# Gated linear attention and a mixture of experts: the first unit in parts, gate steps without a buffer, a carry by a product, constant products at the start, and a table of due times

## The chip, the cores and the metric

The kernel runs on one core of a Trainium2 chip. The core has five engines with a queue each: PE (TensorE: matrix products and transpositions, with weight loads shown as an engine of their own, PEld), DVE (VectorE), ACT (ScalarE, with tables of functions that have to be loaded), POOL (GpSimd) and SP (SyncE, which here only issues transfers). An engine takes its instructions strictly in the order of its queue and waits on semaphores. The metric is the device time of one execution in microseconds (us), the median of several runs.

## The reference

Attention first: for each of 4 batches and 8 heads a complex decay multiplies a 48 x 48 state at each of 768 steps, and k v^T is added to its real part.

```python
mag = np.sqrt(a_re * a_re + a_im * a_im)
scale = np.minimum(mag, 0.999) / (mag + 1e-06)
a_re_n, a_im_n = (a_re * scale, a_im * scale)
for t in range(S):
    new_re = ar * S_re - ai * S_im
    new_im = ar * S_im + ai * S_re
    S_re, S_im = (new_re + kv, new_im)
    y[:, :, t] = np.einsum('bhd,bhde->bhe', q[:, :, t], S_re)
```

The result, as 3072 rows of 384, goes through a layer of 8 experts (384 to 1024 to 384), of which each row uses the one with the largest logit:

```python
logits = x @ w_gate
expert_idx = np.argmax(logits, axis=1)
h = np.maximum(x_sorted[lo:hi] @ w1[e], 0.0)
y_sorted[lo:hi] = h @ w2[e]
return (gate_w[:, None] * y).astype(np.float32)
```

`gate_w` is the softmax probability of the chosen expert. All is float32.

## The kernel before

**Attention.** The 768 steps are cut into 6 units `u` of 128 (NU), which lie on the partitions. A unit has 4 batches (B), so there are 24 pairs g = 4 u + b; a half is two batches (HB). 384 = 8 heads x 48 is one batch's row, 768 a half's, 1536 a unit's. The decay is kept as logarithm and angle. For each unit:

- `load_gates` brings a_re and a_im (`ar`, `ai`), `load_qkv` a half of q, k and v, all from SP.
- `gate_steps` turns them into the clipped logarithm (`ar`) and the ratio (`ai`) in four steps s0 to s3: six passes on ACT (Relu, Ln, Exp, Square, Ln, Exp, all but Relu and Square bound to one ACT table) and four on DVE. Buffers `A` and `R` are single.
- `decay` sums the logarithm over the unit's steps by a product with the triangular matrix `tri` (tile `csl`) and takes its exponential both ways (`E`, `Ei`).
- `angle` takes the arctangent, under the other ACT table. For u > 0 an accumulating transfer from POOL adds the angle at the end of the unit before (`cd`, in DRAM) to row 0. `turns` sums the angles by a product with `tri_turn` (tile `cst`), keeps the fraction of a turn (`fg`), and sends its last row through DRAM, a scaling on DVE and DRAM again to `cd` for the next unit. `rotation` takes sines (`CS`).
- `products` multiplies q and E to `Qe`, k and Ei to `Ke` (a half at a time), and those by CS to `Q` and `K` (a batch at a time).
- `scores(u, b, hg)`, for four heads: transposes K and Q (`tp`), copies them on ACT (`kt`, `qt`), multiplies them (`at`) and masks on DVE (`am`). `outer` forms k v^T (`dk`), `state` carries the state `G` on, `results` forms the output (`yt`) from `am` with v and `qt` with G, `evict` copies it (`ys`), `finish` turns it back (`xb`, with the logits), and stores it to `xd`.

**What sets the order.** Each instruction gets a priority when it is written, `cur_priority`, and a scheduler builds one fixed order for every engine from priorities and dependencies. `put(t, f)` writes f at the due time t, in pairs: `tc.cur_priority = 2000 + int(t * 200)`. Before the change unit 0's gate steps are due from -8, by halves; the decay of unit 0 and all four steps of unit 1 come next, then the table of the angles, then unit 0's turns and sines. In the loop over g, `ahead(g)` places the preparation of unit u + 1 and the first steps of unit u + 2 beside the attention of unit u, with one set of due times for all units; attention's own are products -1.2, scores 0 and 0.3, outer 0.5, results 0.7 and 0.9, evict 1.1, finish 1.3, state 1.5.

**Experts.** `route`, `places` and what follows sort the rows by expert. For each expert `gather` fetches its rows (`xg`, indirect transfers on POOL), `turn` transposes them (`tp`, copied to `xt`), `expert` multiplies with w1 (`hps`, then `ht`) and w2 (`yps`), scales (`y`) and scatters to the output. Weights are loaded two experts ahead by `load_w`. The sizes are the constants CAPS. `in_range` checks that the gates lie where the fast path holds: it loads a_re and a_im once more (`rc`) and compares on DVE (`junk`). `early` runs part of expert 0 under the last unit.

Of the kernel before, what the change touches and what calls it, by code (L numbers as in the profile page):

```python
# [20 lines left out]
P = 128  # L21
# [15 lines left out]
def kernel(  # L37
# [57 lines left out]
    nc.vector.memset(ones, 1.0)  # L95
    mhalfpi = const([P, 1], "mhalfpi")
# [55 lines left out]

    T["ops"] = []

    def act(**kw):

        ins = nc.scalar.activation(**kw)  # L157
        behind(ins, [T["table"]])
        T["ops"].append(ins)

# [7 lines left out]
    def load_gates(u, half):  # L168
        for nm, src in (("ar", a_re), ("ai", a_im)):
            if half == 0:  # L170
                T[nm, u] = ga.tile([P, B, H, D], FP, tag=nm, name=nm)
            sl = slice(half * HB, (half + 1) * HB)
            nc.sync.dma_start(  # L173
                out=T[nm, u][:, sl], in_=src[sl, :, u * P : (u + 1) * P, :].rearrange("b h t d -> t b h d")
            )
# [12 lines left out]
    def gate_steps(u, b0, b1):  # L188

        if b0 == 0:  # L190
            T["A", u] = ga.tile([P, B, H, D], FP, tag="A", name="A", bufs=1)
            T["R", u] = ga.tile([P, B, H, D], FP, tag="R", name="R", bufs=1)
        ar, ai, A, R = (flat(T[nm, u][:, b0:b1]) for nm in ("ar", "ai", "A", "R"))

        def s0():
            act(out=A, in_=ar, func=AF.Relu, bias=a_low)
            act(out=A, in_=A, func=AF.Ln, bias=a_min)

        def s1():
            act(out=R, in_=A, func=AF.Exp, scale=-1.0)  # L200
            tt(out=ai, in0=ai, in1=R, op=OP.mult)
            ts(out=ai, in0=ai, scalar1=-T_MAX, scalar2=T_MAX, op0=OP.max, op1=OP.min)

        def s2():
            act(out=R, in_=ai, func=AF.Square)
            act(out=R, in_=R, func=AF.Ln, bias=1.0)
            stt(out=A, in0=R, scalar=0.5, in1=A, op0=OP.mult, op1=OP.add)

        def s3():
            act(out=R, in_=A, func=AF.Exp, scale=-1.0, bias=ln_eps)  # L210
            stt(out=ar, in0=A, scalar=LN_CAP, in1=R, op0=OP.min, op1=OP.subtract)  # L211
# [3 lines left out]
    def decay(u, half):  # L215

        cs = psC.tile([P, HB, DM], FP, tag="cs", padded_shape=[P, HB, 512], name="csl")
        for c in range(HB):
            mm(cs[:, c], tri, T["ar", u][:, half * HB + c].rearrange("p h d -> p (h d)"))
        for nm, sc in (("E", 1.0), ("Ei", -1.0)):  # L220
            t = ch.tile([P, HB, DM], FP, tag=nm, name=nm, bufs=3)
            act(out=t, in_=cs, func=AF.Exp, scale=sc)
            T[nm, u, half] = t
# [18 lines left out]
    def turns(u, half):  # L242

        fg = un.tile([P, HB, H, 2, D], FP, tag="fg", name="fg")
        T["fg", u, half] = fg
        cs = psC.tile([P, HB, H, D], FP, tag="cs", padded_shape=[P, HB, 8, 64], name="cst")
        prev = T["mm"]
        for c in range(HB):
# [3 lines left out]
        r, f = fg[:, :, :, 0, :], fg[:, :, :, 1, :]  # L252
        ts(out=r, in0=cs, scalar1=MAGIC, scalar2=MAGIC, op0=OP.add, op1=OP.subtract)
        tt(out=f, in0=cs, in1=r, op=OP.subtract)
        fi = fg.bitcast(I32).rearrange("p b h a d -> p (b h) a d")
        ts(out=fi[:, :, 0, :], in0=fi[:, :, 1, :], scalar1=0x7FFFFFFF, scalar2=None, op0=OP.bitwise_and)
        if u + 1 < NU:
# [11 lines left out]
    def rotation(u, half):  # L269

        fg = T["fg", u, half].rearrange("p b h a d -> p (b h) a d")
        CS = un.tile([P, HB * H, 2, D], FP, tag="CS", name="CS", bufs=3)
        act(out=CS[:, :, 0], in_=fg[:, :, 0], func=AF.Sin, scale=2.0 * math.pi, bias=mhalfpi)
        act(out=CS[:, :, 1], in_=fg[:, :, 1], func=AF.Sin, scale=2.0 * math.pi)
        T["CS", u, half] = CS

    def products(u, b):
        half, c = divmod(b, HB)
        for nm, src, dec in (("Q", "q", "E"), ("K", "k", "Ei")):
            if c == 0:  # L280
                e = ch.tile([P, HB * H, D], FP, tag=nm + "e", name=nm + "e", bufs=1)
                tt(
                    out=e.rearrange("p h d -> p (h d)"),
                    in0=flat(T[src, u, half]),
                    in1=T[dec, u, half].rearrange("p b x -> p (b x)"),
                    op=OP.mult,
                )
                T[nm + "e"] = e
# [305 lines left out]
    def expert(i, t0, t1, psH, psO, yp):  # L594
# [14 lines left out]
        for t in range(t0, t1):  # L609
            n = min(P, CAPS[i] - t * P)  # L610
# [30 lines left out]
    def put(t, f, *a):  # L641
        tc.cur_priority = 2000 + int(t * 200)
# [12 lines left out]
    load_qkv(0, 1, "v")  # L655
# [5 lines left out]
    for half in range(2):  # L661
        load_gates(2, half)
    table("natural_log_exp_and_others")
    for i, fs in enumerate(zip(gate_steps(0, 0, HB), gate_steps(0, HB, B))):
        for f in fs:
            put(-8 + i, f)
    for half in range(2):
        put(-4, decay, 0, half)
    for i, fs in enumerate(zip(gate_steps(1, 0, HB), gate_steps(1, HB, B))):
        for f in fs:  # L670
            put(-3, f)
    put(-3, table, "trig_and_small")
    for half in range(2):
        put(-3, angle, 0, half * HB, (half + 1) * HB)
        put(-2.5 + half, turns, 0, half)
    for half in range(2):
        put(-2 + half, rotation, 0, half)
    put(-1, angle, 1, 0, B)

    def ahead(g):  # L680

        u, b = divmod(g, B)
        n, m = u + 1, u + 2
        X = n * B
        if n >= NU:
# [399 lines left out]
```

## Time and profile before

| | us |
|---|---|
| median of 3 runs (588.27, 580.65, 583.8) | 583.8 |
| the profiled execution | 584.5 |
| its span on the core | 582.7 |
| first transposition of K starts | 51.40 |
| first product of expert 0 with all its rows starts | 317.08 |

The span runs from the first instruction to the last and is what the profile divides. One more view is of use, the busy tenths of 40 equal slices of the span (14.6 us each; 9 is 90% or more; PEclk is the clock that TensorE was granted):

```profile
PE   0327999999899999999997999999999999999993
PEld 0114888887788798888775655555555555565651
DVE  3356977868887777776367345302203131110210
ACT  6766978788477665533310110111101011000000
POOL 2000000000000000001044031402213021101001
PEclk9999999999999999999998999999999999999997
```

The first three to four slices are preparation, slices 4 to 19 attention, and from slice 21 on the experts run, with DVE and ACT nearly idle. A busy PE is not PE at its peak: in attention the weight loads (PEld) are busy for 70 to 90% of a slice, in the experts for about half.

### The profile page before, as it was taken

Reading aid. Unit: us, or ns where it says so; the run is one execution under the profiler, and the core shown is the slowest. Engines: PE = TensorE matmul, PEld = TensorE weight load, DVE = VectorE, ACT = ScalarE, POOL = GpSimd, SP = SyncE. Lnnn points to the kernel's source line nnn. Section 1 sums busy time; section 2 is a strip of 40 time slices with the busy share of each in tenths; the row PEclk is TensorE's granted clock in tenths of the full one; section 3 lists DMA queues with packets and bytes.
Section 4 is the critical chain, followed back from the end, with each engine's and each line's share of the span. In section 5 each row is a group of like instructions: output and inputs, shape, how many; then the busy total and the mean of one; then the engine's idle time right before and its main releaser. Section 6 shows DMA issues by size and latency. Waiting matters only on the chain.

```text
span 582.7 us, 8024 instructions
## 1 busy us (share of the span) xinstructions
PE 521.9 (90%) x3133; PEld 365.2 (63%) x3133; DVE 283.6 (49%) x574; ACT 217.8 (37%) x322; POOL 67.3 (12%) x94
## 2 busy tenths in 40 slices
PE   0327999999899999999997999999999999999993
PEld 0114888887788798888775655555555555565651
DVE  3356977868887777776367345302203131110210
ACT  6766978788477665533310110111101011000000
POOL 2000000000000000001044031402213021101001
PEclk9999999999999999999998999999999999999997
DMA  9934574765574737203539985522335232330000
GB/s 167 208 58 56 106 133 89 154 110 110 111 119 76 145 76 139 42 28 105 196 124 355 372 318 229 181 85 69 147 133 164 109 103 92 131 118 28 10 14 28
DMA packets 166727, 73.41 MB, mean 126 GB/s; under 512 B 148398, under 2 KB 159704, under 8 KB 166681
## 3 DMA queue, kind: packets, MB, share of 16 engines
q1 hardware_dynamic: 163096, 63.14, 44.3%
q0 software_dynamic: 3584, 9.68, 4.7%
q8 instruction: 26, 0.43, 0.3%
q14 instruction: 21, 0.16, 0.1%
HBM read 63.27 MB, written 9.74 MB: 125 GB/s over the span
## 4 chain that ended last, share of the span: by engine, by line
PE 81%; SPq 5%; ACT 4%; DVE 4%; DMA 2%; issue 1%; POOL 0%; DVEq 0%; ACTq 0%
PE hps L67 22%; PE yps L67 21%; PE at L67 8%; PE yt L67 7%; PE tp L300 7%; PE dk L67 4%; PE xb L67 4%; PE cst L67 3%; SPq L173 2%; DMA rc<-in_a_im_dram 2%; PE csl L67 2%; SPq L182 2%; PE tp L573 2%; ACT R L157 1%; PE sp L67 1%
## 5 line engine op out<-in xcount | busy, mean ns | idle before, releaser
L67 PE MATMUL hps<-xt,wa 128*128 128x416 f32 (+7 forms) x432 | 134.2, 470 | 2.8 <-DVE xt L580 2.8
L67 PE MATMUL yps<-wb,ht 128*128 128x384 f32 (+6 forms) x464 | 133.9, 487 | 0.0
L67 PEld LDWEIGHTS hps<-xt,wa 128*128 128x128 f32 x432 | 81.2, 194 | 49.8 <-issue 21.3
L67 PEld LDWEIGHTS yps<-wb,ht 128*128 128x128 f32 (+6 forms) x464 | 75.1, 175 | 56.0 <-issue 8.6
L618 DVE TENSOR_SCALAR y<-yps,gate 128x384 f32<-128x384 f32 (+2 forms) x24 | 14.8, 617 | 111.8 <-PE yps L67 111.8
L606 ACT ACTIVATE ht<-hps 128x416 f32<-128x416 f32 (+7 forms) x36 | 16.8, 467 | 131.1 <-PE hps L67 114.3
L67 PE MATMUL at<-qt,kt 96*128 96x128 f32 x384 | 55.0, 283 | 0.7 <-ACT qt L302 0.7
L608 DVE TENSOR_SCALAR ht<-hps 128x416 f32<-128x416 f32 (+7 forms) x36 | 18.9, 525 | 69.8 <-PE hps L67 69.4
L585 POOL DMA_INDIRECT out_dram<-y,row x29 | 29.1, 1005 | 198.5 <-DVE y L618 173.6
L67 PEld LDWEIGHTS at<-qt,kt 96*128 96x128 f32 x384 | 47.8, 191 | 6.6 <-ACT qt L302 2.7
L308 DVE TENSOR_TENSOR am<-at,tri 128x512 f32<-128x512 f32 x48 | 33.0, 687 | 22.8 <-PE at L67 22.7
L67 PE MATMUL yt<-am,v 128*48 128x128 f32 x384 | 40.5, 282 | 3.2 <-DVE am L308 3.0
L67 PE MATMUL csl<-ar,tri 128*128 128x384 f32 x48 | 23.2, 590 | 21.1 <-DVE ar L211 15.6
L554 POOL DMA_INDIRECT xg<-xd,tok x29 | 30.4, 1050 | 94.4 <-PE tp L300 50.1
L302 ACT COPY kt<-tp 96x512 f32<-96x512 f32 x48 | 27.9, 581 | 33.9 <-PE tp L300 33.8
L300 PE MATMUL tp<-ident,K 128*96 128x128 f32 x192 | 35.8, 284 | 2.6 <-ACT kt L302 2.0
L67 PE MATMUL cst<-ai,tri_turn 128*128 128x384 f32 x48 | 21.1, 561 | 15.9 <-ACT ai L157 13.7
L67 PE MATMUL yt<-qt,G 96*48 96x128 f32 x320 | 35.1, 274 | 0.0
L628 ACT COPY z<-yps 32x384 f32<-32x384 f32 (+3 forms) x13 | 6.1, 470 | 73.3 <-PE yps L67 73.3
L67 PE MATMUL dk<-v,K 128*96 128x48 f32 x320 | 31.2, 248 | 0.6 <-DVE G L339 0.6
L67 PEld LDWEIGHTS dk<-v,K 128*96 128x96 f32 x320 | 30.4, 167 | 2.1 <-issue 0.9
L300 PE MATMUL tp<-ident,Q 128*96 128x128 f32 x192 | 31.0, 277 | 0.0
(148 smaller groups left out, 634.2 us busy)
## 6 DMA issues: line engine op xcount, KB each, us to landing
wa<-in_moe_w_dram SPq DMA_DIRECT2D x8, 1536.0 KB, 6.4
wb<-in_moe_w_dram SPq DMA_DIRECT2D x8, 1536.0 KB, 11.5
ar<-in_a_re_dram SPq DMA_DIRECT2D x12, 384.0 KB, 4.6
ai<-in_a_im_dram SPq DMA_DIRECT2D x12, 384.0 KB
q<-in_q_dram SPq DMA_DIRECT2D x12, 384.0 KB, 4.7
k<-in_k_dram SPq DMA_DIRECT2D x12, 384.0 KB, 4.4
v<-in_v_dram SPq DMA_DIRECT2D x12, 384.0 KB, 4.8
xd<-x SPq DMA_DIRECT2D x24, 192.0 KB, 3.8
```

The lines of the kernel that those rows point to most:

```text
L67: T["mm"] = nc.tensor.matmul(o, lhsT=lhsT, rhs=rhs, start=start, stop=stop, skip_group_check=True)
L173: nc.sync.dma_start(out=T[nm, u][:, sl], in_=src[sl, :, u * P : (u + 1) * P, :].rearrange("b h t d -> t b h d"))
L182: nc.sync.dma_start(out=t, in_=src[sl, :, u * P : (u + 1) * P, :].rearrange("b h t d -> t b h d"))
L300: nc.tensor.transpose(out=tp[0:DD, j], in_=X[:, hg * 4 + j], identity=ident)
L302: nc.scalar.copy(out=t[0:DD], in_=tp[0:DD])
L308: tt(out=am, in0=at, in1=bc(tri, 1, 4), op=OP.mult)
L554: nc.gpsimd.indirect_dma_start(out=T["xg", i][0:n, t], out_offset=None, in_=xd[0:rows, :], in_offset=bass.IndirectOffsetOnAxis(ap=tok[0:n, ...
L573: ins = nc.tensor.transpose(out=tp[:, (t - t0) * P : (t - t0) * P + n], in_=xg[0:n, t, d * P : (d + 1) * P], identity=ident[0:n, 0:n],)
L585: nc.gpsimd.indirect_dma_start(out=out, out_offset=bass.IndirectOffsetOnAxis(ap=row[0:n, i, t : t + 1], axis=0), in_=y[0:n], in_offset=Non ...
L606: nc.scalar.activation(out=ht[:, f, c0:c1], in_=ps, func=AF.Relu)
L608: ts(out=ht[:, f, c0:c1], in0=ps, scalar1=0.0, scalar2=None, op0=OP.max)
L618: ts(out=y[0:n], in0=ps[0:n], scalar1=g, scalar2=None, op0=OP.mult)
```

## The change

1. Unit 0 is loaded and prepared in three parts: batch 0, batch 1, half 1. `decay`, `turns`, `rotation` and `products` take a range of batches. In unit 0 a maximum on DVE replaces the Relu on ACT (`c0`); later units keep the Relu.
2. `gate_steps` works in `ar` and `R` (two buffers); `A` is gone, `Square` stands in s1 and is not bound to a table. `E` and `Ei` have four buffers instead of three.
3. Unit 1's carry is a product of `last` (ones in its last row) with unit 0's `fg`, accumulated into `cst`. Units 2 to 5 keep the way through DRAM.
4. `warm` writes 40 products of `tri` with itself ahead of unit 0's turns, in ten groups that each wait for an ACT pass.
5. The table `WHEN` gives each piece a due time for each unit, relative to the unit's first pair, and `put` starts at 4000.
6. In the experts, `turn(i + 1)` is written within `expert(i)`, ahead of its last two tiles of `yps`, and the second expert's weights are loaded ahead of its gather.

```diff
+    last = const([P, P], "last")
+    nc.gpsimd.affine_select(
+        out=last, in_=ones, pattern=[[0, P]], base=-(P - 1), channel_multiplier=1, compare_op=OP.is_ge, fill=0.0
+    )
...
+    def warm(n):
+
+        w = psX.tile([P, P], FP, tag="xb", padded_shape=[P, 512], name="warm")
+        for i in range(n):
+            ins = mm(w, tri, tri)
+            if i == 0:
+                tc.add_manual_dep(ins.ins, T["act"].ins.name, SYNC, reason="pace")
...
-            T["A", u] = ga.tile([P, B, H, D], FP, tag="A", name="A", bufs=1)
-            T["R", u] = ga.tile([P, B, H, D], FP, tag="R", name="R", bufs=1)
-        ar, ai, A, R = (flat(T[nm, u][:, b0:b1]) for nm in ("ar", "ai", "A", "R"))
+            T["R", u] = ga.tile([P, B, H, D], FP, tag="R", name="R", bufs=2)
+        ar, ai, R = (flat(T[nm, u][:, b0:b1]) for nm in ("ar", "ai", "R"))
 
         def s0():
-            act(out=A, in_=ar, func=AF.Relu, bias=a_low)
-            act(out=A, in_=A, func=AF.Ln, bias=a_min)
+            if T["when"](f"c{u}"):
+                ts(out=R, in0=ar, scalar1=A_MIN, scalar2=None, op0=OP.max)
+                act(out=ar, in_=R, func=AF.Ln)
+            else:
+                nc.scalar.activation(out=R, in_=ar, func=AF.Relu, bias=a_low)
+                act(out=ar, in_=R, func=AF.Ln, bias=a_min)
 
         def s1():
-            act(out=R, in_=A, func=AF.Exp, scale=-1.0)
+            act(out=R, in_=ar, func=AF.Exp, scale=-1.0)
             tt(out=ai, in0=ai, in1=R, op=OP.mult)
             ts(out=ai, in0=ai, scalar1=-T_MAX, scalar2=T_MAX, op0=OP.max, op1=OP.min)
+            T["act"] = nc.scalar.activation(out=R, in_=ai, func=AF.Square)
...
-        if u > 0:
+        if u > 1:
             nc.gpsimd.dma_start(
...
-        for c in range(HB):
-            mm(cs[:, c], tri_turn, T["ai", u][:, half * HB + c].rearrange("p h d -> p (h d)"))
+        for c in range(c0, c1):
+            mm(cs[:, c], tri_turn, T["ai", u][:, half * HB + c].rearrange("p h d -> p (h d)"), True, u != 1)
             if u > 0:
                 behind(T["mm"], [prev])
+            if u == 1:
+                mm(cs[:, c], last, T["fg", 0, half][:, c, :, 1], False, True)
...
-        if u + 1 < NU:
+        if 0 < u < NU - 1:
...
+            if t == t1 - 2 and between is not None:
+                between()
...
+    WHEN = {
+        "l1": 0, "l2": 1, "p0": 2, "p1": 4, "p2": 4, "p3": 2, "p4": 4, "p5": 3, "s0.0.0": -8.68, "c0": True,
...
+        "results0": 1.02, "results1": 1.04, "state": 1.61, "evict": 1.11, "scores0": -0.86, "scores1": 0.42,
+        "outer": 0.43, "finish": 1.53, "products": -1.42, "LE2": -6.28, "d2.0": -3, "d2.1": 0.0, "h3": False,
...
-    load_gates(0, 0)
-    load_gates(0, 1)
-    load_gates(1, 0)
-    load_gates(1, 1)
-    load_qkv(0, 0, "qk")
-    load_qkv(0, 1, "qk")
-    load_qkv(0, 0, "v")
-    load_qkv(0, 1, "v")
+    HS = [(0, HB), (HB, B)]
+    for b0, b1 in ((0, 1), (1, HB), (HB, B)):
+        load_gates(0, b0, b1)
+    order = [(load_qkv, 0, 0, "qk"), (load_qkv, 0, 0, "v"), (load_qkv, 0, 1, "qk"), (load_qkv, 0, 1, "v")]
+    order.insert(when("l1"), (load_gates, 1, 0, HB))
+    order.insert(when("l2"), (load_gates, 1, HB, B))
...
+    turn(0, EARLY, tiles(0), psG)
+    load_w(1, T["turned"])
     for i in range(E):
         t0 = EARLY if i == 0 else 0
-        turn(i, t0, tiles(i), psG)
         if i + 1 < E:
             gather(i + 1, 0, tiles(i + 1))
-        if i == 0:
-            load_w(1, T["turned"])
-        expert(i, t0, tiles(i), psH, psO, yp)
+        expert(i, t0, tiles(i), psH, psO, yp, (lambda: turn(i + 1, 0, tiles(i + 1), psG)) if i + 1 < E else None)
```

**Where instructions stand now.** PE from the start of the program, before (the first row is the branch that starts the queue; `x4` is four in a row):

```order
L1080 UNCONDITIONAL_BRANCH
L67 MATMUL csl<-ar,tri 128x384 x4
L67 MATMUL cst<-ai,tri_turn 128x8x48 x4
L67 MATMUL csl<-ar,tri 128x384 x2
L300 MATMUL tp<-ident,K 96x128 x4
L300 MATMUL tp<-ident,Q 96x128 x4
L67 MATMUL dk<-v,K 96x48 x8
```

The same place after:

```order
L67 MATMUL warm<-tri 128x128 x3
L67 MATMUL csl<-ar,tri 128x384
L67 MATMUL warm<-tri 128x128 x5
L67 MATMUL csl<-ar,tri 128x384
L67 MATMUL warm<-tri 128x128 x32
L67 MATMUL cst<-ai,tri_turn 128x8x48 x4
L326 MATMUL tp<-ident,K 96x128 x4
L326 MATMUL tp<-ident,Q 96x128 x4
```

Of the six `csl` products ahead of the first transposition two are left, for unit 0's first half; the other four stand behind it, and the constant products are new. On ACT, around the first table of sines, before (`ai<-ai` is the arctangent, `CS<-fg` a sine; `A<-A,a_min` to `R<-A,ln_eps` are unit 1's gate steps):

```order
L157 ACTIVATE A<-A,a_min 128x768 x2
L157 ACTIVATE R<-A 128x768 x2
L157 ACTIVATE R<-ai 128x768 x2
L157 ACTIVATE R<-R 128x768 x2
L157 ACTIVATE R<-A,ln_eps 128x768 x2
L162 ACT_TABLE_LOAD
L157 ACTIVATE ai<-ai 128x768 x2
L157 ACTIVATE ai<-ai 128x1536
L157 ACTIVATE CS<-fg 128x16x48
```

And after, where copies for attention stand between the sines:

```order
L175 ACT_TABLE_LOAD
L169 ACTIVATE ai<-ai 128x384
L218 ACTIVATE R<-ai 128x768
L169 ACTIVATE ai<-ai 128x384
L169 ACTIVATE ai<-ai 128x768
L169 ACTIVATE ai<-ai 128x1536
L169 ACTIVATE CS<-fg,mhalfpi 128x8x48
L169 ACTIVATE CS<-fg 128x8x48 x2
L328 COPY kt<-tp 96x512
L328 COPY qt<-tp 96x512
L169 ACTIVATE CS<-fg,mhalfpi 128x8x48
L328 COPY kt<-tp 96x512
```

The last two steps (s2, s3) of unit 0's second half and of unit 1, with their `csl` products and exponentials, moved from ahead of the first transposition to behind it. PE within unit 2, before (numbers tell tiles apart; `at_1343` is masked to `am_1348`):

```order
L300 MATMUL tp_1439<-ident_65,K_1416 96x128 x4
L67 MATMUL at_1343<-qt_1341,kt_1334 128x128 x4
L300 MATMUL tp_1446<-ident_65,Q_1412 96x128 x4
L67 MATMUL yt_148<-am_1348,v_763 48x128 x2
L67 MATMUL yt_148<-qt_1341,G1_944 48x128 x2
```

After, a place of the same kind (`at_1206` is masked to `am_1211`):

```order
L326 MATMUL tp_1213<-ident_65,K_1169 96x128 x4
L67 MATMUL at_1206<-qt_1204,kt_1197 128x128 x4
L326 MATMUL tp_1220<-ident_65,Q_1165 96x128 x4
L67 MATMUL yt_150<-am_1211,v_825 48x128
L326 MATMUL tp_1353<-ident_65,K_1330 96x128 x4
L326 MATMUL tp_1360<-ident_65,Q_1328 96x128 x4
L67 MATMUL at_1227<-qt_1225,kt_1218 128x128 x4
L67 MATMUL yt_150<-am_1211,v_825 48x128
```

The pair's transpositions now run further ahead of the results, so that other products stand between `at` and the `yt` that need its mask. DVE where the early part of expert 0 ends (`junk` is the range check, two passes to a check), before:

```order
L618 TENSOR_SCALAR y_3081<-yps_3080,gate_154 128x384
L580 COPY xt_3026<-tp_3136 128x192
L777 SCALAR_TENSOR_TENSOR junk_3411,inr_3135<-rc1_3408,rc0_3407 128x1536 x2
L777 SCALAR_TENSOR_TENSOR junk_3567,inr_3135<-rc1_3564,rc0_3563 128x1536
L618 TENSOR_SCALAR y_3095<-yps_3094,gate_154 128x384
L580 COPY xt_3026<-tp_3144 128x192
```

After:

```order
L647 TENSOR_SCALAR y_3140<-yps_3139,gate_156 128x384
L606 COPY xt_3085<-tp_3195 128x192
L860 SCALAR_TENSOR_TENSOR junk_3489,inr_3194<-rc1_3486,rc0_3485 128x1536 x2
L647 TENSOR_SCALAR y_3154<-yps_3153,gate_156 128x384
L606 COPY xt_3085<-tp_3203 128x192
```

The first pass of the second check moved from ahead of the copy to `xt` to behind it. PE at the boundary of experts 4 and 5, before:

```order
L67 MATMUL yps_3824<-wb_3561,ht_3755 128x384 x8
L67 MATMUL yps_3838<-wb_3561,ht_3755 16x384 x8
L573 MATMUL tp_3880<-ident_65,xg_3745 128x128 x3
L573 MATMUL tp_3885<-ident_65,xg_3745 128x128 x3
L573 MATMUL tp_3890<-ident_65,xg_3745 128x128 x3
L67 MATMUL hps_3906<-xt_3879,wa_3715 128x384 x3
```

After:

```order
L599 MATMUL tp_3884<-ident_65,xg_3804 128x128 x3
L599 MATMUL tp_3889<-ident_65,xg_3804 128x128 x3
L67 MATMUL yps_3899<-wb_3639,ht_3814 128x384
L599 MATMUL tp_3894<-ident_65,xg_3804 128x128 x3
L67 MATMUL yps_3899<-wb_3639,ht_3814 128x384 x7
L67 MATMUL yps_3913<-wb_3639,ht_3814 16x384 x8
L67 MATMUL hps_3965<-xt_3883,wa_3793 128x384 x3
```

The transpositions of the next expert's rows stand ahead of the last two tiles of `yps`.

More of the change, by code (lines that the diff above doesn't have):

```diff
@@ L660 @@
             )
[L661 to L675, printed above, removed]
@@ L680, in ahead, with sine @@
+    def sine(n):
+        X = n * B
+        put(X + when(f"TR{n}"), table, TR)
+        if not ANG.get(n):
+            put(when(f"a{n}") + X, angle, n, 0, B)
+        for half in range(2):
+            put(X + when(f"t{n}.{half}"), turns, n, half)
+            put(X + when(f"r{n}.{half}"), rotation, n, half)
+        if n + 1 < NU and STEPS[n] > 1:
+            ANG[n + 1] = True
+            put(X + 4 + when(f"a{n + 1}"), angle, n + 1, 0, B)
     def ahead(g):
         u, b = divmod(g, B)
-        n, m = u + 1, u + 2
@@ L684, in ahead @@
[L684 to L708 removed]
+        n = u + 1
@@ L710, in at @@
+        if n < NU and b == 0:
+            log_exp(n)
+        if n < NU and b == (0 if n == 1 else 1):
+            if u in GROUPS:
+                put(n * B + when(f"g{u}"), T["second"])
+            sine(n)
     def at(t, f, g, *a):
@@ L712, in at @@
             put(g + t, f, *divmod(g, B), *a)
-    at(-1.2, products, 0)
     at(0, scores, 0, 0)
```

180 lines of the change are left out of this document (108 added, 72 removed), and 16 rows, old and new, of the table WHEN.

## The prediction

> **What bounds the kernel now.** I read the page's first part, then busy time by stretch (columns: stretch and length; busy us and count of PE, weight loads PEld, DVE, ACT, POOL; granted clock; DMA share; GB/s). The cuts are the first transposition, the second unit's first K product and the end of attention; the last row is one dense slice.
>
> ```profile
> span 582.7 us, 8024 instructions
> PE 521.9 (90%) x3133; PEld 365.2 (63%) x3133; DVE 283.6 (49%) x574; ACT 217.8 (37%) x322; POOL 67.3 (12%) x94
> ```
>
> ```profile
> 0.00:51.40 51.40, 14.34 (x20) 6.07 (x21) 24.42 (x40) 32.16 (x38) 3.52 (x31) 1.00 0.94 138
> 51.40:84.00 32.60, 31.02 (x265) 26.46 (x263) 24.88 (x34) 27.72 (x38) 1.09 (x1) 1.00 0.56 93
> 84.00:287.10 203.10, 195.81 (x1852) 165.11 (x1852) 152.00 (x306) 130.26 (x188) 5.24 (x6) 1.00 0.52 109
> 204.00:224.00 20.00, 20.00 (x216) 18.35 (x214) 15.56 (x38) 11.25 (x19) 0.76 (x1) 1.00 0.39 75
> ```
>
> For 51.4 us PE has almost nothing; ACT, the busiest, prepares two units of gates. From 51.4 to 84 ACT is busy 85% and DVE 76%: they feed the first unit. After that PE is first in line. Next the timeline at the start (start, duration, engine, line, operation, idle time before).
>
> ```profile
> 4.92 0.93 ACT L157 ACTIVATE A<-ar,a_low 128x768 f32<-128x768 f32 x1 [2.91 <-DMA ar<-in_a_re_dram]
> 7.72 0.96 DVE L201 TENSOR_TENSOR ai<-ai,R 128x768 f32<-128x768 f32 x1 [5.47 <-ACT R L157]
> 8.94 0.55 DVE L202 TENSOR_SCALAR ai<-ai 128x768 f32<-128x768 f32 x1
> 19.67 0.79 ACT L157 ACTIVATE E<-csl 128x768 f32<-128x768 f32 x1
> 20.36 0.80 ACT L157 ACTIVATE Ei<-csl 128x768 f32<-128x768 f32 x1
> 35.63 1.28 ACT L162 ACT_TABLE_LOAD   x1
> 42.98 2.90 PE L67 MATMUL cst<-ai,tri_turn 128*128 128x384 f32 x4 [2.24 <-DVE fg L254]
> 51.40 1.06 PE L300 MATMUL tp<-ident,K 128*96 128x128 f32 x4
> 83.12 0.94 DVE L291 TENSOR_TENSOR K<-CS,Ke 128x768 f32<-128x768 f32 x1
> ```
>
> The last row is the K product of pair 4 (second unit, first batch). It is the yardstick: in both orders the same preparation lies behind it (gates of unit 2 done, those of unit 3 not begun).
>
> **Term 1, the first unit in parts.** Prices, by form:
>
> ```profile
> L157 ACT ACTIVATE R<-A 128x1536 f32<-128x1536 f32 x4 | 6.0, 1491 | 0.0
> L157 ACT ACTIVATE R<-A 128x768 f32<-128x768 f32 x4 | 3.3, 840 | 0.1
> L302 ACT COPY kt<-tp 96x512 f32<-96x512 f32 x48 | 27.9, 581 | 33.9 <-PE tp L300 33.8
> L157 ACT ACTIVATE E<-csl 128x768 f32<-128x768 f32 x12 | 9.7, 812 | 4.5 <-PE csl L67 4.4
> ```
>
> 768 more elements cost ACT 0.65 us, so a pass over 384 is about 0.52 us (estimate). Ahead of the first batch's sines ACT now has 18 passes of 384, 12 of 768, one of 1536 and one table load: 18 x 0.5 + 12 x 0.85 + 1.5 + 1.3 = 22.0. A load of half the size should land about 1 us sooner than at 4.9, and the maximum that replaces the Relu is on DVE: start 4.3. Three waits for a pair of DVE passes (as 7.72 and 8.94 show them, about half as long) add 2.5: sines done at about 29. DVE, with two Ke parts and the second batch's turns ahead, then makes Q and K at 0.94 each: first transposition at 32, 19 us earlier. The load order, the added mask on POOL and the loads of unit 2 behind the second half's turns on SP are covered by that wait: no one needs them before 40.
>
> But work stays behind it. From 29.4 to the sines of pair 4 ACT's order holds 20 copies (0.58 less the 0.1 by which neighbours overlap: the E pass at 19.67 takes 0.79, and the next starts 0.69 later), 3 copies of 384 elements (0.37 by the slope above), six E and Ei at 0.71, sines 4.0 (two of 384, four of 768), six passes of 768 at 0.8, six of 1536 at 1.43, two table loads 2.6: 9.6 + 1.1 + 4.3 + 4.0 + 4.8 + 8.6 + 2.6 = 35.0 us. At the 80% to which ACT and DVE fill the stretch they bound (85 and 76 above) this takes 43.7: sines at 73.1, then two DVE products and a queue of about 1: K of pair 4 at 76 instead of 84 (83.12 and 0.94). **Gain 8.** Filled wholly: 66 + 2, a gain of 16. Filled to 70%: 79.4 + 3, a gain of 2. I keep the middle, since the same engines bound both stretches.
>
> PE gets four products with `last` and four csl that used to lie ahead of 51.4. A cst or csl is two records of 0.32 us, by the chain that ended last:
>
> ```profile
> 79.18 1.29 PE cst L67 x4
> 61.41 0.87 PE tp L300 x8
> ```
>
> 8 x 0.64 = 5.1 us, costed at nothing: PE waits for ACT there. Were that cover gone, up to 5. The carry by product removes two round trips through DRAM for unit 1, which nothing waited for: 0. The 40 constant products run on an idle PE; they hold cst back only if they last past 25: 0. One step less on ACT (Relu to DVE) is in the count; it holds for unit 0 alone, later units still run the Relu. Square without a table dependence and buffer A move no pass: 0.
>
> In the rows above the clock is granted at 1.00, yet four cst records took 2.90 us at 42.98 and 1.29 at 79.18. The Trainium skill (TensorE: Matmul & The Clock Gate, What's actually happening) has an idle array at half rate until about 3.4 us of activity. The trace agrees on the factor (2.2); by that rule the constant products save up to 0.8 us at each early cst, by the row at 42.98 (cold again after 2.24 us) nothing. The sum takes nothing.
>
> **Term 2, due times in the middle (84 to 287).** No work goes. What the order can win is waits of PE's weight loads:
>
> ```profile
> PEld yt L67 <- DVE am L308: 4.3, 7, 1.1
> PEld tp L300 <- ACT kt L302: 3.3, 7, 0.9
> PEld xb L67 <- ACT ys L345: 2.7, 4, 1.2
> PEld at L67 <- ACT qt L302: 1.7, 9, 0.3
> PE hps L67 <- DVE xt L580: 2.8, 1, 2.8
> ```
>
> The columns are us in total, times and the longest; the first four are of this stretch alone and come to 12.0 us, the fifth is of the experts. Counted in PE's rows at the rates above, 8 of the 40 masked products from unit 1 on had under 1 us of products between `at` and the first `yt` that needs the mask, now 3; for `at` behind its transpositions 10 of 40, now 4. That is about half of them: **gain 6**. Upper end: the whole stretch as dense as 204:224, 18.35 us of weight loads in 20; 165.11 / 0.92 = 180, a gain of 23. Lower end: the 5.1 us of term 1 without cover, a loss of 5. I take 6, nearest the rows of the waits.
>
> The Trainium skill (Perfetto Trace Analysis, Identifying the Most-Contended Engine) judges TensorE by weight loads, not by matmul busy time. By matmul busy time (195.81 of 203.10) at most 7 us were to be had, by weight loads 23; the four waits above, 12 us, agree with the skill.
>
> **Term 3, the experts.** Two places. First the chain that ended last:
>
> ```profile
> 314.46 1.77 DVE junk L777 x2
> 316.23 0.53 DVE y L618
> 316.76 0.27 DVE xt L580
> 317.08 9.04 PE hps L67 x44
> ```
>
> Then two boundaries between experts, from the timeline:
>
> ```profile
> 369.11 2.13 PE L573 MATMUL tp<-ident,xg 128*128 128x128 f32 x12
> 371.17 1.31 PE L67 MATMUL hps<-xt,wa 128*128 128x416 f32 x3
> ...
> 540.83 0.78 PE L573 MATMUL tp<-ident,xg 128*128 128x128 f32 x6
> ...
> 542.58 0.79 PE L67 MATMUL hps<-xt,wa 128*128 128x360 f32 x2
> ```
>
> The range check `junk` stood ahead of y and xt on DVE and waited for its load; now it stands behind. Of the 2.8 us, 0.4 remain for the two copies: 2.4. At each later boundary PE transposes, waits for copies, then starts hps: 371.17 - 369.11 = 2.06 for 12 transpositions that need 1.31 at 0.109; 1.75 for 9 that need 0.98 at the last one. About 0.75 at each of seven, 5; now they stand ahead of the last yps tiles, whose time covers the copies. I keep 4.6. **Gain 7**, with 5 and 8 as ends. w1's load now precedes the gather and leaves earlier: 0, since hps waits for xt alone in the rows above.
>
> **Sum.** Span 582.7, this execution 584.5, the median of three runs 583.8 (580.65 to 588.27), 0.7 less. 584.5 - 8 - 6 - 7 = 563.5, about **563** for the median.
>
> **Rivals.** (a) Postponed, not saved: first unit +2 only, the added products uncovered, so the middle gives about 2: 584.5 - 2 - 2 - 7 = 573.5. For it: ACT and DVE have 35 us to do where they had 28. Against: 20 us are then free for it. (b) Denser: 584.5 - 8 - 18 - 7 = 551. For it the slice 204:224; against, the stretch as a whole holds 16.3 in 20 (165.11 of 203.10). (c) Slower, by the carry: each unit's cst stands in PE's row behind an accumulating DMA.
>
> ```profile
> 106.49 0.80 POOL L236 DMA_DIRECT2D ai<-cd  x1 [36.27 <-PE xb L67]
> 112.97 1.46 PE L67 MATMUL cst<-ai,tri_turn 128*128 128x384 f32 x4
> ai<-cd POOLq DMA_DIRECT2D x5, 6.0 KB, 3.9
> ```
>
> 106.49 + 3.9 = 110.4, 2.6 us to spare. SP's row now has the first carry of a unit behind ai, ar, k and v loads that wait for PE. Each us beyond 2.6 stops PE once in units 2 to 5: from (21 + 10.4) / 4, 8 us late, it undoes the 21 us; at 9 late, 588. Against: about as much DVE work stands between the carry's scaling and cst as before.
>
> **How the numbers follow.** My forecast, 557 to 570: 0.54. (b) 0.11. (a) 0.28, half of it on either side of 572. (c) 0.07, of which 0.05 slower. The range 553 to 576 leaves out (c), the denser half of (b) and the top of (a), under 0.2. Two per cent, 11.7 us, is about what a measurement of this kernel can tell: faster 0.54 + 0.11 + 0.13 = 0.78, within 0.17, slower 0.05.
>
> **What would show it.** First transposition near 32; K of pair 4 near 76; attention's last xb near 273, not 287; no wait of hps for xt in the experts; transpositions inside yps. Wrong: K of pair 4 after 82, PE idle ahead of cst in units 2 to 5, or ACT under 75% between 32 and 76.

## The result, and the profile after

The changed kernel took 566.0 us (median of 4 runs, 564.15 to 567.8) beside 582.2 for the kernel before: a ratio of 0.970, with a 95% interval of 0.962 to 0.979. Measured again beside the experiments it took 563.5 against 583.9: 0.966 (0.962 to 0.969). The profiled execution took 564.15, 20.3 us less than the one of before; its span is 20.8 us shorter.

The page's first part and three rows of its slices (14.0 us each):

```profile
span 561.9 us, 8229 instructions
PE 529.7 (94%) x3221; PEld 376.7 (67%) x3221; DVE 286.5 (51%) x584; ACT 217.8 (39%) x330; POOL 68.8 (12%) x94
...
PE   3889979999999999999899999999999999999993
...
ACT  6867988786588764553201010101101011010100
PEclk9979999999999999999999999999999999999998
```

From the second slice on PE is busy for eight tenths or more, but for one 7 and the end (most of the constant products lie in the second). ACT does the same work (217.8 us in both). New is a 7 in the third slice of the granted clock. Busy time by stretch, with the columns of the prediction's rows, cut at the first transposition, the end of pair 4's K product and the end of attention:

```profile
0.00:33.05 33.05, 20.17 (x92) 14.49 (x93) 17.93 (x40) 22.41 (x34) 4.00 (x32) 0.93 1.15 167
33.05:79.05 46.00, 41.64 (x321) 33.31 (x319) 35.97 (x47) 37.94 (x50) 0.00 (x0) 0.98 0.67 104
79.05:271.70 192.65, 189.24 (x1812) 163.38 (x1813) 150.49 (x301) 129.64 (x187) 5.54 (x6) 1.00 0.55 114
```

The points that answer to those of before, from the timeline:

```profile
33.05 1.06 PE L326 MATMUL tp<-ident,K 128*96 128x128 f32 x4
...
78.10 0.95 DVE L317 TENSOR_TENSOR K<-CS,Ke 128x768 f32<-128x768 f32 x1
...
270.59 1.14 PE L67 MATMUL xb<-back,ys 128*128 128x104 f32 x8 [0.69 <-ACT ys L371]
...
298.93 8.07 PE L67 MATMUL hps<-xt,wa 128*128 128x192 f32 x48
```

The first transposition starts 18.35 us earlier (51.40 before), K of pair 4 5.0, the last `xb` of attention 15.65 (286.24 before), and the first `hps` with all of expert 0's rows 14.5 (in the trace before it starts at 313.40, and PE stops from 314.3 to 317.08, which is the time that the table ahead of the prediction gives for it). From there to the end it is 269.3 us before and 263.0 now.

Such times can differ by chance. The run experts_only (below) has the same start as the kernel before, and its first transposition comes at 50.00: there four `cst` records took 1.60 us that took 2.90 in the trace of before (the prediction's row at 42.98):

```profile
42.88 1.60 PE L67 MATMUL cst<-ai,tri_turn 128*128 128x384 f32 x4 [2.24 <-DVE fg L254]
```

K of pair 4 is a poor yardstick, since PE can be ahead with other work when it comes. A better one is the count of PE's products. This table is worked out from the starts of PE's records in the traces, without the constant products and those with `last`; it gives when the kernel before starts the product of that number, and how much earlier another kernel does (the three on the right are told below). The last row is near the end of attention.

| product | before, us | changed | old_middle | old_start | old_both |
|---|---|---|---|---|---|
| 20 | 50.8 | -16.2 | -16.2 | -2.3 | -1.7 |
| 260 | 81.6 | -17.3 | -12.7 | -3.9 | -0.7 |
| 380 | 95.0 | -9.6 | -8.2 | -1.7 | -1.7 |
| 980 | 163.6 | -11.2 | -6.3 | -3.2 | -4.8 |
| 2100 | 282.3 | -14.1 | -4.8 | -5.1 | -5.0 |

How much earlier a kernel is may be called its lead. The changed kernel's is 16 to 17 us at first, 7.7 of it go between 64 and 86 us, then 4.5 are won on the way to the end of attention. Where the 7.7 go, the chain that ended last shows:

```profile
65.58 2.65 PE cst L67 x8
68.23 0.89 PE at L67 x8
69.13 0.87 PE xb L67 x8
70.00 1.01 PE yt L67 x16
71.01 2.79 PE cst L67 x8
73.80 0.02 issue
73.82 0.96 DVE fg L277
74.78 1.67 DVE ar L226
76.45 0.87 DVE fg L278
...
78.10 0.95 DVE K L317
```

Unit 1's two `cst` groups have 8 records each, four of them products with `last`. They stand on the chain, and so does one pass of unit 2's gate steps (`ar`, 1.67 us) that DVE's order puts between the two passes of `fg`. Meanwhile PE stops. These are the stretches of products 260 to 380, in the changed kernel and before:

```profile
64.40:85.50 21.10, 17.24 (x131) 13.51 (x131) 18.32 (x23) 18.09 (x22) 0.00 (x0) 1.00 0.82 130
```

```profile
81.60:95.00 13.40, 12.75 (x121) 11.08 (x122) 10.03 (x16) 11.72 (x15) 0.00 (x0) 1.00 0.49 93
```

PE is idle for 3.9 us of the first and for 0.65 of the second, and the products with `last` take some 2.7. The rest is that unit 1's other `cst`, long records, lay ahead of product 260 in the kernel before.

### The profile page after: what moved, and what is told of

The parts are those of the page before. It is cut to its first block, busy times and chain, and to the rows that moved or that the text cites. A ratio compares the mean times of both kernels' runs of the same rounds, so it can differ in the third digit from the quotient of the medians.

```text
span 561.9 us, 8229 instructions
## 1 busy us (share of the span) xinstructions
PE 529.7 (94%) x3221; PEld 376.7 (67%) x3221; DVE 286.5 (51%) x584; ACT 217.8 (39%) x330; POOL 68.8 (12%) x94
## 4 chain that ended last, share of the span: by engine, by line
PE 81%; DVE 6%; ACT 5%; DMA 4%; issue 2%; POOL 0%; ACTq 0%; DVEq 0%
PE yps L67 23%; PE hps L67 23%; PE tp L326 7%; PE at L67 6%; PE yt L67 6%; PE cst L67 4%; PE dk L67 3%; PE xb L67 3%; PE csl L67 2%; PE tp L599 2%; DMA xd<-x 2%; DMA xg<-xd,tok 1%; ACT R L169 1%; PE sp L67 1%; DVE ai L216 1%
## 5 line engine op out<-in xcount | busy, mean ns | idle before, releaser
L67 PE MATMUL yps<-wb,ht 128*128 128x384 f32 (+6 forms) x464 | 136.8, 489 | 0.0
L67 PE MATMUL hps<-xt,wa 128*128 128x416 f32 (+7 forms) x432 | 132.4, 465 | 0.0
L611 POOL DMA_INDIRECT out_dram<-y,row x29 | 29.4, 1014 | 195.2 <-DVE y L647 166.9
L334 DVE TENSOR_TENSOR am<-at,tri 128x512 f32<-128x512 f32 x48 | 33.0, 688 | 20.8 <-PE at L67 20.5
L67 PE MATMUL yt<-am,v 128*48 128x128 f32 x384 | 43.0, 281 | 0.6 <-DVE am L334 0.6
L580 POOL DMA_INDIRECT xg<-xd,tok x29 | 32.0, 1104 | 77.5 <-PE tp L326 40.3
L67 PE MATMUL yt<-qt,G 96*48 96x128 f32 x320 | 36.7, 274 | 0.0
L326 PE MATMUL tp<-ident,K 128*96 128x128 f32 x192 | 33.0, 283 | 1.8 <-ACT kt L328 0.9
L326 PE MATMUL tp<-ident,Q 128*96 128x128 f32 x192 | 32.9, 277 | 0.0
L67 PEld LDWEIGHTS yt<-am,v 128*48 128x48 f32 x384 | 24.8, 122 | 8.2 <-DVE am L334 2.2
L255 POOL DMA_DIRECT2D ai<-cd x4 | 3.4, 842 | 211.9 <-ACT R L169 100.5
L328 ACT COPY qt<-tp 96x512 f32<-96x512 f32 x48 | 28.1, 586 | 2.9 <-PE tp L326 2.9
```

What stands on the lines that cost most here:

```text
L67: T["mm"] = nc.tensor.matmul(o, lhsT=lhsT, rhs=rhs, start=start, stop=stop, skip_group_check=True)
L326: nc.tensor.transpose(out=tp[0:DD, j], in_=X[:, hg * 4 + j], identity=ident)
L328: nc.scalar.copy(out=t[0:DD], in_=tp[0:DD])
L334: tt(out=am, in0=at, in1=bc(tri, 1, 4), op=OP.mult)
L580: nc.gpsimd.indirect_dma_start(out=T["xg", i][0:n, t], out_offset=None, in_=xd[0:rows, :], in_offset=bass.IndirectOffsetOnAxis(ap=tok[0:n, ...
L611: nc.gpsimd.indirect_dma_start(out=out, out_offset=bass.IndirectOffsetOnAxis(ap=row[0:n, i, t : t + 1], axis=0), in_=y[0:n], in_offset=Non ...
```

## The experiments

### The parts alone: theory I, and what it was tried against

Theory I is the prediction's: three parts (start, middle's due times, experts) whose gains add. Rival II: the early start alone is worth nothing. Rival III: it is worth all.

**experts_only**: the kernel before, with the change's loop over the experts.

```diff
+            if t == t1 - 2 and between is not None:
+                between()
...
+    turn(0, EARLY, tiles(0), psG)
+    load_w(1, T["turned"])
...
+        expert(i, t0, tiles(i), psH, psO, yp, (lambda: turn(i + 1, 0, tiles(i + 1), psG)) if i + 1 < E else None)
```

> The kernel before with the change in the experts alone: the next expert's transpositions ahead of the last two yps tiles, w1 of expert 1 ahead of its gather. Theory I (the gain is a sum of three parts that don't touch one another: start 9, middle 5, experts 6, against 582): 576, hps no longer waits 2.8 us for xt at the first boundary, and 0.5 us less at each later one. Rival (the wait at the first boundary is not the order but the late transfer of rows or checks, which falls on something else): 579 to 580, only the later boundaries gain.

**old_start**: the changed kernel with unit 0 in halves and the start's due times of before.

```diff
+    for i, fs in enumerate(zip(gate_steps(0, 0, HB), gate_steps(0, HB, B))):
+        for f in fs:
+            put(-8 + i, f)
+    for half in range(2):
+        put(-4, decay, 0, half)
+    for i, fs in enumerate(zip(gate_steps(1, 0, HB), gate_steps(1, HB, B))):
+        for f in fs:
+            put(-3, f)
...
+    put(-3, table, TR)
```

> The changed kernel, but with unit 0 loaded and prepared by halves in the order and with the due times of before, all of unit 1's gate steps ahead of the first table of sines, the Relu on ACT, no constant products; the due times of units 1 to 5 and of attention and the experts as changed. Theory I: 571 to 573 (9 to 10 us slower than the changed kernel measured beside the kernel before), first transposition near 51, the middle as dense as in the changed kernel. Rival II (the start alone is worth nothing, the gain of attention is from the middle's due times): 566 to 568. Rival III (all of attention's gain is the earlier start): 576.

**old_middle**: the changed kernel with the due times of before for the preparation of units 2 to 5, and for attention's own pieces in every unit.

```diff
+    for n in range(2, NU):
+        WHEN.update({f"p{n}": 4, f"LE{n}": -4.2, f"d{n}.0": -2.5, f"d{n}.1": -2, f"TR{n}": -2.4, f"h{n}": False})
+        WHEN.update({f"t{n}.0": -3, f"t{n}.1": -2, f"r{n}.0": -1.8, f"r{n}.1": -1})
+        if n > 2:
+            WHEN.update({f"s{n}.0.0": -8, f"s{n}.0.1": -7.7, f"s{n}.0.2": -7.4, f"s{n}.0.3": -7, f"a{n}": -4.5})
+    WHEN.update({"g2": -3, "g4": -3})
+    WHEN.update({"products": -1.2, "results0": 0.7, "results1": 0.9, "evict": 1.1, "finish": 1.3, "state": 1.5})
+    WHEN.update({"scores0": 0, "scores1": 0.3, "outer": 0.5})
```

> The changed kernel, but units 2 to 5 are prepared at the due times of before (one set for all) and attention's pieces have theirs too; unit 0 in parts, unit 1's own times and the experts as changed. Theory I: 567 (start 9 and experts 6 of 582 kept, middle 5 lost). Rival II: 574 to 576. Rival III: 562 to 564, no slower than the changed kernel.

**old_both**: both edits.

> The changed kernel with the start of before and the middle's due times of before: what is left is the experts, the missing buffer, Square without a table, a fourth buffer of E and Ei, the carry of unit 1 by a product, and unit 1's own due times. Theory I: 576, as the experts alone. Rival (the buffers and Square are worth something by themselves): 571 to 573.

Beside 583.5 for the kernel before:

| | us | ratio (95% interval) |
|---|---|---|
| experts_only | 582.6 | 0.998 (0.996 to 1.001) |
| old_both | 576.2 | 0.987 (0.983 to 0.991) |
| old_middle (new start, old due times) | 576.6 | 0.988 (0.985 to 0.992) |
| old_start (old start, new due times) | 574.0 | 0.984 (0.980 to 0.987) |
| changed kernel (measured again, later) | 563.5 | 0.966 (0.962 to 0.969) |

The gains do not add. With the due times of before the early start is worth nothing (0.987 and 0.988): rival II holds there. With the late start the new due times are worth 0.3%, within both intervals; old_start's 574.0 lies between what theory I and rival III gave. Together they are worth 2.1%, from 0.987 to 0.966. That old_both came at the 576 of theory I is luck: the theory had it from the experts alone, which are worth 0.2% (below).

The table of products shows how: in old_middle the early start is there (16 us at 20 products) and leaks away to 5 near the end of attention, where old_start and old_both are 5 ahead too, while in the changed kernel 9.6 become 14.1. So 9 us of the 10 to 13 between old_both and the changed kernel are attention's. The rest lies mostly in expert 0: from its first `hps` to that of expert 1 it is 20.81 us in old_both and 19.77 in old_middle, but 17.24 in old_start and the changed kernel, by DVE's order, as told below. PE's waits for the four copies and masks of the prediction's term are 5.9 us in the changed kernel's middle, against 12.0 before (transpositions for `kt`, `xb` for `ys`, `yt` for `am`, `at` for `qt`):

```profile
PEld tp L326 <- ACT kt L328: 2.4, 4, 1.1
PEld xb L67 <- ACT ys L371: 1.9, 2, 0.9
...
PEld yt L67 <- DVE am L334: 1.2, 4, 0.6
...
PEld at L67 <- ACT qt L328: 0.4, 2, 0.2
```

From experts_only to old_both lies another 1.2%. It comes of the buffers, the free Square, unit 1's carry and its own due times with the old start, or of the order that they bring (1.4 us of it is in expert 0, 22.23 against 20.81); these were not taken apart.

The loop over the experts by itself moved 0.2% at most, where 6 us were expected. Two things explain it. First, at the boundaries of 416 and 408 rows there was no wait to remove. A transposition of `xg` takes 0.164 us, as the eight and four of the changed kernel show, which stand inside `yps` and wait for nothing:

```profile
343.35 1.31 PE L599 MATMUL tp<-ident,xg 128*128 128x128 f32 x8
...
345.34 0.68 PE L599 MATMUL tp<-ident,xg 128*128 128x128 f32 x4
```

Twelve take 1.97 of the 2.06 us. From the first `hps` of one expert to that of the next it is 35.9 us in both kernels for experts 1 and 2; only before the last three experts 0.4 to 0.6 us are saved, 1.6 in all. Second, the 3 us wait ahead of expert 0 stayed. PE and then DVE in experts_only, from the timeline:

```profile
316.13 9.10 PE L67 MATMUL hps<-xt,wa 128*128 128x192 f32 x44 [3.04 <-DVE xt L580]
```

```profile
313.51 1.76 DVE L779 SCALAR_TENSOR_TENSOR junk<-rc,rc 128x1536 f32<-128x1536 f32 x1 [3.57 <-DMA rc<-in_a_im_dram]
```

The second check still stood ahead of `xt` on DVE and waited for its load.

### Is it DVE's order?

**checks_behind**: experts_only, with the checks ordered behind the last copy to `xt`. Order alone, without a wait.

```diff
+    T["first"] = T["turned"]
...
+            behind(ins, [T["first"]])
```

> The experts-only kernel with one thing more: the range checks (junk) stand on DVE behind the last copy to xt of expert 0, by an order without a wait; apart from them the queues are the same. Theory: the wait at expert 0 is DVE's order alone (3.04 us at 316.13, and the 44 products behind it took 9.10 where the changed kernel has 8.07 for 48, 1.7 more): 4.7 faster than the experts-only kernel, 578, that is 0.991 of the kernel before. Rival (the checks' transfers are late anyway, and their delay falls on ht or y behind them): 581 to 583.

It took 577.0 beside 582.9: 0.990 (0.987 to 0.993), 5 us less than experts_only, as expected. PE there:

```profile
312.19 8.07 PE L67 MATMUL hps<-xt,wa 128*128 128x192 f32 x48
```

The wait is gone, and 48 products take 8.07 us where 44 took 9.10 behind it: 3.0 us are the wait, 1.7 the slower products. So it is the order. The slower products are a matter of the clock, which is granted at 0.50 for 3.4 us just behind the wait (experts_only, the number behind POOL's), and half of 3.4 is 1.7:

```profile
317.30:320.70 3.40, 3.40 (x13) 3.40 (x12) 3.40 (x7) 0.33 (x1) 1.54 (x2) 0.50 0.96 345
```

The changed kernel has the same 8.07, though nothing in its text orders the checks: its schedule happened to put them there (old_both and old_middle, with the same loop, still wait 1.63 and 2.26 us).

### The carry by a product

**dram_carry**: the changed kernel with unit 1's carry through DRAM.

```diff
-        if u > 1:
+        if u > 0:
...
-            if u == 1:
-                mm(cs[:, c], last, T["fg", 0, half][:, c, :, 1], False, True)
...
-        if 0 < u < NU - 1:
+        if c1 == HB and u < NU - 1:
```

> The changed kernel, but unit 1's carry goes through DRAM as before and the products with last are gone. Theory A (PE is on the path between 60 and 80 us, where unit 1's two cst groups of 8 records took 2.65 and 2.79 us): 2.7 faster than the changed kernel, 0.966 of the kernel before, and the work is up to 19 us ahead there. Rival B (the round trip is late now that the first unit is early): slower by 3 or more, PE or DVE waiting ahead of unit 1's cst. Rival C (neither, the difference is that of another order of the queues): within 2.

It took 581.0 beside 582.9: 0.996 (0.994 to 0.999), 15.0 and 17.5 us slower than the changed kernel's two measurements: rival B, and by far more than its 3. The chain of waits (this trace is of the slowest of its twelve executions, 585.15):

```profile
67.12 0.69 DVE am L333
67.81 0.09 DVE carry L289
...
67.92 2.47 DMA cd<-carry
...
70.40 2.98 DMA carry<-cd
...
73.71 1.53 DMA cd<-carry
...
75.94 4.47 DMA ai<-cd
...
80.45 2.73 PE cst L67 x4
```

The carry's scaling stands on DVE behind an `am`, and the second half's load comes behind the first half's store (they share the one buffer `carry`), so from this scaling to the last landing it is 67.8 to 80.4: 12.6 us. Busy time around it:

```profile
68.30:95.00 26.70, 12.75 (x57) 9.29 (x56) 13.89 (x17) 13.45 (x14) 1.08 (x1) 0.64 0.76 134
```

PE is idle for 13.95 us, and its clock is granted at 0.64 on top. The lead of 16.7 us at product 260 has become a lag of 5.2 at 380, and a lag it stays (2.3 at 2100). The changed kernel loses 7.7 us of its lead in the same place, so the difference there is 14. The queues of this kernel also stand in another order, which may account for the rest.

### The constant products

**no_warm**: the changed kernel without them. **warm_half**: 64 columns instead of 128, with the same queues as no_warm but for them.

```diff
-            put(when(f"w{i}"), warm, 4)
...
-            ins = mm(w, tri, tri)
+            ins = mm(w[:, 0:64], tri, tri[:, 0:64])
```

> The changed kernel without the 40 constant products (the queues of all engines change with that in some 60 places). Theory: they save at most 0.7 us ahead of each of the first two pairs of cst, of which 0 to 1 us reaches the end; the rest is order: 0.968 to 0.977 of the kernel before. Rival (the clock they keep up is worth more): the first transposition 2 us later than 33.05 and the end 2 us or more later than in the run with products of half the width.

> The changed kernel with the 40 constant products at 64 columns instead of 128: all five queues are the same as in the run without them, but for these products. So this pair shows what they are worth with one order. Theory: within 1 us of the run without them. Rival: 2 us or more faster.

no_warm took 574.4 beside 582.9, 0.985 (0.982 to 0.989): slower than the changed kernel by more than was expected. warm_half took 580.3, 0.993 (0.990 to 0.996): 6 us slower than no_warm with the same order, against both theories. The timeline of PE says why, first no_warm, then warm_half:

```profile
24.91 1.65 PE L67 MATMUL cst<-ai,tri_turn 128*128 128x384 f32 x2 [10.26 <-ACT ai L169]
```

```profile
21.15 10.07 PE L67 MATMUL warm<-tri 128*128 128x64 f32 x40 [0.91 <-ACT R L218]
31.01 1.59 PE L67 MATMUL cst<-ai,tri_turn 128*128 128x384 f32 x2
```

A record of 64 columns takes 0.25 us. One of 128 columns takes 0.28 at first and then 0.15 in the changed kernel:

```profile
11.77 2.83 PE L67 MATMUL warm<-tri 128*128 128x128 f32 x10
...
15.14 9.63 PE L67 MATMUL warm<-tri 128*128 128x128 f32 x64
```

So PE became fast behind the wide products and not behind the narrow ones. The narrow ones held the first `cst` back by 6 us, and did not speed it up: 1.59 against 1.65, where the changed kernel has 0.91. The Trainium skill (TensorE: Matmul & The Clock Gate, What's actually happening) has the array leave its slow state after about 3.4 us of sustained activity. The changed kernel's 0.91 agrees; warm_half does not, since ten unbroken microseconds of narrow products left it slow.

Since the order of no_warm differs from that of the changed kernel in some 60 places, two more kernels keep the changed kernel's order. **warm_28** leaves out the group at the first gate step, **warm_60** has six products in a group.

```diff
-            put(when(f"w{i}"), warm, 4)
+            put(when(f"w{i}"), warm, 4) if i != 0 else None
...
+            put(when(f"w{i}"), warm, 6)
```

> The changed kernel once more, beside the three variants that follow. 0.966 to 0.974 of the kernel before (it was 0.970): about 566 against 583.

> The changed kernel with 28 constant products instead of 40 (the three groups at the first gate step are gone); all other instructions of all queues stand as in the changed kernel. Theory (the products are worth something because the dip of the granted clock that follows the first stretch of PE work, 0.82 and 0.50 at 25 to 35 us in the changed kernel, then lies ahead of the first transposition, where in the run without them it lay at 45 to 60): with fewer of them the dip comes later and costs 2 to 4 us, 568 to 570. Rival (only the order of the queues differed between those runs): within 1 us of the changed kernel.

> The changed kernel with 60 constant products, the last six of them between the first two cst products, all else in the same order. Theory: the dip ends before the first transposition or at it, 0 to 2 us faster than the changed kernel, 564 to 566. Rival (they hold back the first unit's cst, and PE's queue with it): the first transposition after 34 us, 1 to 3 us slower.

| constant products | us | ratio (95% interval) |
|---|---|---|
| 28 | 563.8 | 0.966 (0.962 to 0.970) |
| 40, changed_again | 563.5 | 0.966 (0.962 to 0.969) |
| 60 | 565.4 | 0.969 (0.966 to 0.973) |

With one order their number is worth nothing that can be told: the rival of warm_28 holds. For warm_60 neither side does: it is not faster, and its first transposition comes at 33.77. The clock did move as the theory had it. Windows of the changed kernel and of warm_60 (the number behind POOL's is the granted clock):

```profile
25.00:35.00 10.00, 6.71 (x18) 3.85 (x19) 8.12 (x15) 5.79 (x9) 0.00 (x0) 0.66 0.67 108
```

```profile
25.00:35.00 10.00, 8.19 (x55) 6.18 (x53) 8.46 (x16) 6.73 (x11) 0.00 (x0) 1.00 0.58 100
```

With 60, PE comes to product 260 only 0.1 us sooner than with 40, and to 2100 it comes 1.0 later.

### How much hangs on the order

**nudge**: one due time, `"finish": 1.53`, becomes 1.45.

> The changed kernel with one due time moved a little (finish at 1.45 instead of 1.53), which changes the order of PE in 114 places and names nothing that any theory holds to be dear. Theory (the order within the middle is worth some 3 us either way, and the rest of the change holds by itself): 563 to 570. Rival (the gain hangs on this one order, as the losses of 8 and 15 us without the constant products and without the carry by product could be read): 573 or more.

It took 569.1 beside 583.9: 0.974 (0.971 to 0.978), 5.6 us slower than the changed kernel, without a product or a transfer more. So another order of the middle can cost 6 us, more than the 3 that were expected, and less than the losses of no_warm and dram_carry. Part of it is again the clock: behind a stop of PE of 3.51 us, where the changed kernel has one of 2.76, it is granted at half in nudge and at 1.00 in the changed kernel:

```profile
78.40:85.30 6.90, 5.40 (x18) 3.59 (x18) 5.68 (x7) 6.86 (x8) 0.00 (x0) 0.51 1.08 174
```

Since PE is busy for 5.40 us there, that costs up to some 2.7 (an estimate). No kernel here was faster than the changed one. What nudge shows limits the runs above, too: each of old_start, old_middle, no_warm and dram_carry is one order among many, so differences of 6 us between them can come of that alone. The 9 us that attention gains from both parts together, and the 14 of the carry, are more, but each rests on one such pair.

## Why the prediction was right, point by point

- **The total, 563 against 566.0 and 563.5: right**, and for part of its reasons only. The three sizes came near (8, 6 and 7 against 9.6, 4.5 and 6.3), but they are not three independent terms, and that two parts of the change could be put at 0 holds only for the order that was built. In that the total is in part luck.
- **Term 1, 8 us.** The first transposition was put at 32 and came at 33.05; ACT's first pass, put at 4.3 from a load that lands a microsecond sooner, came at 4.65. K of pair 4 was put at 76 and came at 79.05: between the two ACT was busy for 37.94 of 46.00 us, 82%, near the 80 assumed. By that yardstick the gain is 5.0; by PE's products it is 9.6, of which 1.4 is the slow `cst` in the trace of before. The term is right in size, its yardstick was not good. (Its upper end doesn't follow from its own figures: filled wholly, 29.4 + 35.0 is 64.4, not 66.) Wrong was "costed at nothing: PE waits for ACT there" for the products with `last`: unit 1's `cst` are on the chain, 5.4 us with `last`, about half of that without, and PE's cover was gone there.
- **The carry by a product, 0.** Wrong. The step that failed is "two round trips through DRAM, which nothing waited for", read from the order of before. In the order of dram_carry the way through DRAM takes 12.6 us and starts late, and the lead is lost there.
- **The constant products, 0.** Right with the order kept (28, 40 and 60 within 2 us). The reading of the row at 42.98 as "cold again after 2.24 us" is no rule: in experts_only the same four records come behind the same 2.24 us and take 1.60. Without them the scheduler makes another order, and that cost 8 us or more beside the kernel before (0.985 against 0.966 or 0.970). Its lead falls from 18.9 us at product 100 to 7.6 at 260, between 44 and 74 us (the changed kernel's from 19.6 to 17.3), and the clock was 0.54 from 45 to 60. PE was busy for 12.35 us of these, so the clock can have cost up to some 6 (an estimate); no run separates it from the order.
- **Term 2, 6 us.** The waits it counted went from 12.0 to 5.9, as said, and the lead grew by 4.5 from product 380 on. But it is not a term of its own: with the old start it is worth 0.3%, with the new one 11 to 13 us (576.6 to 566.0 or 563.5), some 9 of them in attention. Rival (a), the lead only postponed, is what the kernel does with the due times of before.
- **Term 3, 7 us.** 6.3 came (269.3 to 263.0), in other places. The first wait was put at 2.4 and is worth 4.6 with the slower products behind it (from expert 0's first `hps` to expert 1's it is 21.85 us before and 17.24 now), 1.7 of it by the clock; the other boundaries were put at 4.6 and give 1.6, because a transposition of 128 by 96 (0.109) was taken for one of 128 by 128 (0.164). And the edit of the loop doesn't remove the first wait; the order that the scheduler found does.
- **Rival (c)**, PE stopped by the accumulating transfer in units 2 to 5, did not come: the waits of the changed kernel's middle show no `cst` behind it. In unit 1, with the carry put back, it came just so.

## What to carry to other kernels

An early start is a loan: it is kept only if every later stage is ordered for it, so measure it together with the due times, and follow the lead by products done, not by one event. Where a scheduler makes the order, every edit is also another order, and one that changed nothing else cost 6 us (1%) here: compare variants whose queues are the same (28, 40, 60 products), or state an order where it matters, as for the checks, where that gave 0.8%. And a price is taken from a row of the same shape.

## What had not been expected of the hardware

- The granted clock falls to half for some 3 to 14 us, and where that falls differs: at 28.3 to 35.0 us in the changed kernel and at 46.1 to 59.8 in no_warm (0.50 in both), nowhere between 15 and 557 us in warm_60 (1.00). Of no_warm:

```profile
45.00:60.00 15.00, 12.35 (x49) 9.22 (x49) 10.98 (x14) 7.17 (x12) 0.00 (x0) 0.54 0.64 92
```

  It can be dear: warm_half took 575.0 and 575.2 us in the two runs with a mean clock of 0.991 and 0.992, and 578 to 581 in the ten with 0.979 to 0.985. In the kernel before it is not: of its 23 runs beside that one, the eight above 0.985 have a median of 583.7 us, the fourteen below 0.98 one of 582.6.
- Narrow products did not bring PE up to speed here: behind 80 records of 64 columns, the last 40 of them unbroken, two `cst` records still took 1.59 us; in the changed kernel, behind the first 16 records of 128 columns and two `csl`, the next two `csl` took 0.91.
- Behind a stop of 1.6 to 3 us, 44 products of expert 0 took 9.0 to 9.1 us (before, experts_only, old_both) instead of 7.4 (8.07 for 48); behind one of 2.26 in old_middle they took 7.42. In the three the granted clock is 0.50 for 3.4 us there; in old_middle it is not:

```profile
308.00:322.00 14.00, 11.74 (x66) 10.19 (x67) 9.84 (x16) 1.83 (x5) 8.27 (x6) 1.00 0.96 341
```

  What decides which stop the clock follows is open: it fell behind one of 1.63 us and not behind the changed kernel's 2.76.
